# float64 weights converted by two bit operations and an integer addition, with one pair of heads masked on VectorE

## The chip, the cores and the metric

One core of a Trainium2 chip. The metric is the device time of one execution in microseconds. A core has five engines with queues of their own: TensorE (PE; its weight loads are listed as PEld), VectorE (DVE), ScalarE (ACT), GpSimd (POOL) and SyncE (SP).

## What is computed

Hashed attention, and behind it a Fourier mixing block, cut to what matters:

```python
# attention: B, H, S, D = 4, 8, 768, 64; float32
q_bits = einsum('bhsd,dk->bhsk', q, proj) > 0          # 6 bits; k_bits alike
mask   = q_bucket[:, :, :, None] == k_bucket[:, :, None, :]
scores = where(mask, q @ k.T / sqrt(D), -1e9)
attn   = exp(scores - max); attn = attn / (sum(attn) + 1e-09)
x      = (attn @ v), heads side by side: (4, 768, 512)
# mixing
u  = x + real(fft(fft(x, axis=1), axis=2))
un = (u - mean) / sqrt(var + 1e-06)
out = u + maximum(un @ w_ch1, 0.0) @ w_ch2             # (512, 2048) and (2048, 512)
```

`w_ch1` and `w_ch2` arrive as float64 (a float32 array times a float64 scalar); the rest is float32. The kernel is handed their 64-bit words and turns them into float32 itself.

## The kernel before, in words

**Attention.** Heads are taken in 16 pairs (`NPAIR` = 4 for each of 4 batches); a pair has six steps, one for each block of 128 keys (`NT` = 6). In each step `weigh` (L775 on) runs twice, for the two halves of the queries: TensorE computes scores of both heads (L789), ScalarE takes the exponential (L795) into one of four buffers `pk`. Then VectorE adds the new probabilities to the accumulators (L868), and TensorE multiplies the step before with the values (L809). After a pair, `scale` sums over the keys (L826) and divides on VectorE (L832 to L842).

The mask of equal buckets comes in one of two ways. For pairs in `LITE` (L541) the score matmul is led by two bf16 matmuls (L784) on the signs of the bits, scaled by 2^34, so that other buckets' exponentials vanish; the signs are prepared by wide matmuls (L727) and VectorE (L729, L734), and the copies of the transposed q and k all go to ScalarE (`act`, L692). For all other pairs `prepare` computes bucket numbers with narrow matmuls (L742, L754, L763), whose results go through score buffers in PSUM and are copied by VectorE and ScalarE in turn, and `weigh` multiplies each probability by "bucket of q equals bucket of k" on VectorE, two operations in a half step (L798). `prepare(n + 1)` runs inside pair n.

**Weights.** `weights` (L612) brings a 512-column slice at a time: 16 slices for w1 and 16 for w2. A slice's raw words are loaded (seven buffers for w1, three for w2; later loads are issued on GpSimd's queue, L636, when a buffer is free), then `narrow` (L581) converts it: three ScalarE operations make a mask of the values whose exponent fits float32 (L589 to L591), five VectorE operations shift the high word into place, set the exponent and sign, and turn the low word into a float remainder (L595, L598, L601, L605, L607), and GpSimd adds the remainder (L610). High and low words are read with a step of two. For w1, GpSimd also adds up four slices (L657), TensorE takes the mean (L670), and VectorE subtracts it (L673).

**Order.** In batch 0 the order of PE, DVE, ACT and POOL is that of the program (`manual_schedule`, L1034 on): one slice of w1 after each attention step, so the 16 slices lie in pairs 0 to 2. From batch 1 on a scheduler orders the instructions by its own costs; three steps of the mixing of the batch before follow each attention step, and from the eleventh mixing step of batch 0 on, slices of w2 alternate with mixing steps (L1065), during pairs 4 and 5.

**Mixing.** Per batch: sums and differences (L906, L910), channel transform (L923 and the copies L928, L930), sequence transform (L949, L965), two matmul layers (L974 with evictions L981 and L983; L1002), normalisation (L990 to L999) and stores (L893).

**The flag.** In the last batch the largest norms of q and k are reduced, transposed and compared (L1050 to L1060); if the exponentials could overflow, the kernel is followed by a general, slower version, `_any_scores`. With the given data it isn't run.

Of the kernel before, what the change touches and what calls it, by code (L numbers as in the profile page):

```python
# [23 lines left out]
DFF = 4 * DM  # L24
# [5 lines left out]
NDC = DM // P  # L30
GTT = 2
GT = GTT * P
WC = 512

SCALE = 1.0 / float(np.sqrt(D))
# [7 lines left out]
SAFE = 36.0  # L43
# [422 lines left out]
def _main(  # L466
# [9 lines left out]
    cn: dict,  # L476
):

    nc = tc.nc

    const = ctx.enter_context(tc.tile_pool(name="const", bufs=1))
# [11 lines left out]
    def wt(shape, dtype, tag, name, bufs=2):  # L493
        return work.tile(shape, dtype, tag=tag, name=name, bufs=bufs)
# [43 lines left out]
    make_identity(nc, ident)  # L538


    LITE = (0, 1, 2, 3, 4)  # L541
    pjw = const.tile([P, P], F32, tag="pjw", name="pjw")
    nc.gpsimd.memset(pjw, 0.0)
    for h in range(2):
# [15 lines left out]
    norms = const.tile([P, 2, NPAIR * B], F32, tag="norms", name="norms")  # L560
# [12 lines left out]
    w1 = const.tile([P, NDC, DFF], F32, tag="w1", name="w1")  # L573
# [7 lines left out]
    def narrow(dst, raw, mask):  # L581


        lo, hi = (raw.rearrange("p (n w) -> p n w", w=2)[:, :, i] for i in range(2))
        di, mi = dst.bitcast(I32), mask.bitcast(I32)

        nc.scalar.activation(mask, hi, AF.Abs)  # L589
        nc.scalar.activation(mask, mask, AF.Abs, bias=mid[:, 0:1])  # L590
        nc.scalar.activation(mi, mask, AF.Sign, bias=mid[:, 1:2])  # L591

        nc.vector.tensor_scalar(  # L595
            di, hi, 4, -(2**31), op0=ALU.logical_shift_left, op1=ALU.bitwise_xor
        )
        nc.vector.scalar_tensor_tensor(  # L598
            mi, di, 1, mi, op0=ALU.logical_shift_right, op1=ALU.bitwise_and
        )  # L600
        nc.vector.scalar_tensor_tensor(  # L601
            di, hi, -(2**31), mi, op0=ALU.bitwise_and, op1=ALU.bitwise_or
        )

        nc.vector.tensor_scalar(mi, di, -(1 << 23), None, op0=ALU.bitwise_and)  # L605
        rest = lo.bitcast(F32)
        nc.vector.scalar_tensor_tensor(  # L607
            rest, lo.bitcast(U32), 2.0**-52, mask, op0=ALU.mult, op1=ALU.mult
        )
        nc.gpsimd.tensor_tensor(dst, dst, rest, op=ALU.add)  # L610

    def weights(wsb, wdr):  # L612

        wide = wdr.dtype == I64
        slices = [
            (wsb[:, c, f : f + WC], wdr[c * P : (c + 1) * P, f : f + WC])
            for f in range(0, wdr.shape[1], WC)
            for c in range(wdr.shape[0] // P)
        ]
        raws, masks, adding = [], [], []  # L620
        if wide:
            zt = wt([P, 3, 2 * WC], F32, "z", f"zraw{wdr.shape[0]}", 1)
            raws += [zt[:, i] for i in range(3)]
            if wsb is w1:
                ft = wt([P, 12, WC], F32, "F", "fraw", 1)
                raws += [
                    ft[:, i : i + 2].rearrange("p i w -> p (i w)") for i in range(0, 8, 2)
                ]
                masks = [ft[:, i] for i in range(8, 12)]

        def fetch(i, queue):
            if i < len(slices):
                dst, src = slices[i]
                if wide:
                    raw = raws[i % len(raws)].bitcast(I32)
                    queue.dma_start(raw.bitcast(I64), src)  # L636
                else:
                    queue.dma_start(dst, src)

        depth = len(raws) or 4  # L640
        for i in range(depth):
            fetch(i, nc.sync if wsb is w1 else nc.gpsimd)
            if wsb is w1 and i == 1:
                load(1)
        yield
        for i, (dst, src) in enumerate(slices):
            if wide:
                mask = masks[i % 4] if masks else wt([P, WC], F32, "u", f"mask{i}", 2)
                narrow(dst, raws[i % len(raws)].bitcast(I32), mask)
# [37 lines left out]
    def prepare(n):  # L687

        lite = n in LITE
        act = lite and n > 0  # L692
# [349 lines left out]
    for b in range(B):  # L1042
        if b > 0:
            for _ in attention(b):
                for _ in range(per_step):
                    next(other, None)
        if b == B - 1:
            roomy[0] = True

            ms = const.tile([P, 2], F32, tag="ms", name="ms")  # L1050
            nc.vector.tensor_reduce(ms, norms, axis=AX.X, op=ALU.max)
            ps = pt([1, 2, P], "norms_t")
            for io in range(2):
                nc.tensor.transpose(ps[:, io, :], ms[:, io : io + 1], ident)
            mt = const.tile([1, 4], F32, tag="mt", name="mt")
            nc.vector.tensor_reduce(mt[:, 0:2], ps, axis=AX.X, op=ALU.max)
            nc.vector.tensor_tensor(mt[:, 2:3], mt[:, 0:1], mt[:, 1:2], op=ALU.mult)
# [55 lines left out]
```

## Time and profile before

| what | value |
|---|---|
| time, median of 3 runs | 1313.91 us (1313.45 to 1316.85) |
| the profiled execution | 1313.88 us, span 1312.0 us |
| PE busy | 1229.4 us (94%) |
| DVE busy | 691.7 us (53%) |
| ACT busy | 347.4 us (26%) |
| POOL busy | 138.1 us (11%) |
| moved by DMA | 44.65 MB, mean 34 GB/s |

Busy times overlap, as the engines run side by side, so they don't add up to the span. The page also gives the span in 40 slices, each digit the busy share in tenths. A row of a group gives line, engine, operation, output and inputs, shapes and count, then busy time, mean time of one in ns, and the idle time before with what ended it. A row of a stretch gives its start and end, its length, and for each engine the busy time and the number of instructions, then TensorE's granted clock (1.00 is full), the DMA share and GB/s.

### The profile page before, as it was taken

What the parts mean: (1) busy time and instruction counts of PE and PEld (TensorE: products, weight loads), DVE (VectorE), ACT (ScalarE), POOL (GpSimd) and SP (SyncE); (2) the same over time, 40 slices, a digit from 0 to 9 for tenths busy, and PEclk for the clock granted to TensorE, in tenths of its full rate; (3) what the DMA queues carried; (4) which work ended last, traced back from release to release, by engine and by line L of the source; (5) the groups of instructions that cost most, each with busy time, mean ns of one, the idle gap of its engine ahead of it and who ended that gap; (6) DMA issues with size and microseconds to landing.
All of it is one profiled execution on the core that took longest, in us unless ns stands there. A gap on an engine that the chain in (4) does not pass through costs nothing.

```text
span 1312.0 us, 12075 instructions
## 1 busy us (share of the span) xinstructions
PE 1229.4 (94%) x4688; PEld 619.9 (47%) x4688; DVE 691.7 (53%) x1184; ACT 347.4 (26%) x569; POOL 138.1 (11%) x183
## 2 busy tenths in 40 slices
PE   7657889899999999999999999999999998999997
PEld 3223356344445445644445444745445444854553
DVE  5999967994444448553444537653444635310010
ACT  6446444551122214122122213122112111110000
POOL 1443202430000100000100110000000000001000
PEclk9778999899999999999999999999999998999999
DMA  9321112330100101010110101010000000000000
GB/s 286 88 72 36 37 37 94 111 89 8 32 20 13 32 8 45 1 24 12 28 33 0 35 18 33 12 24 13 17 21 0 0 12 13 0 0 16 8 8 19
DMA packets 82881, 44.65 MB, mean 34 GB/s; under 512 B 76800, under 2 KB 76928, under 8 KB 82688
## 3 DMA queue, kind: packets, MB, share of 16 engines
q1 hardware_dynamic: 74032, 23.61, 7.2%
q0 software_dynamic: 5648, 19.40, 4.6%
q10 hardware_dynamic: 3136, 0.79, 0.3%
q8 instruction: 39, 0.64, 0.2%
q14 instruction: 26, 0.21, 0.1%
HBM read 37.50 MB, written 6.29 MB: 33 GB/s over the span
## 4 chain that ended last, share of the span: by engine, by line
PE 75%; DVE 17%; issue 4%; ACT 2%; DMA 1%; POOL 1%; SPq 0%; POOLq 0%; DVEq 0%; ACTq 0%
PE o L1002 24%; PE h L974 23%; PE sc L789 8%; PE oo L809 7%; DVE acc L868 4%; PE cs L923 3%; DVE pk L798 3%; PE B L949 2%; PE A L949 2%; DVE w L601 1%; PE sum L826 1%; DVE fraw L598 1%; ACT pk L795 1%; DVE zraw L607 1%; PE un L990 1%
## 5 line engine op out<-in xcount | busy, mean ns | idle before, releaser
L974 PE MATMUL h<-x,w 128*128 128x384 f32 x1024 | 344.4, 493 | 11.5 <-DVE rt L832 3.5
L1002 PE MATMUL o<-w,h 128*128 128x512 f32 x768 | 342.1, 597 | 0.4 <-DVE h L981 0.4
L974 PEld LDWEIGHTS h<-x,w 128*128 128x128 f32 x1024 | 192.1, 191 | 159.2 <-issue 12.8
L798 DVE SCALAR_TENSOR_TENSOR pk<-qb,kb,pk 128x384 f32<-128x384 bf16 x264 | 155.7, 628 | 189.3 <-ACT pk L795 189.3
L795 ACT ACTIVATE pk<-sc 128x768 f32<-128x768 f32 x192 | 149.2, 809 | 327.6 <-PE sc L789 250.6
L1002 PEld LDWEIGHTS o<-w,h 128*128 128x128 f32 x768 | 141.5, 190 | 174.2 <-issue 168.0
L789 PE MATMUL sc<-qt,kt 64*128 64x384 f32 x768 | 186.4, 518 | 2.8 <-ACT pk L795 2.8
L809 PE MATMUL oo<-pk,vn 128*64 128x384 f32 (+1 forms) x768 | 152.9, 500 | 1.7 <-ACT x L821 1.1
L868 DVE TENSOR_TENSOR acc<-acc,pk 128x768 f32<-128x768 f32 x128 | 134.9, 1063 | 5.2 <-ACT pk L795 3.4
L981 DVE TENSOR_SCALAR h<-h 128x384 f32<-128x384 f32 x64 | 35.6, 556 | 166.4 <-PE h L974 166.2
L789 PEld LDWEIGHTS sc<-qt,kt 64*128 64x128 f32 x768 | 77.5, 193 | 75.3 <-issue 49.9
L983 ACT ACTIVATE h<-h 128x384 f32<-128x384 f32 x64 | 31.4, 491 | 284.3 <-PE h L974 284.3
L1008 DVE SCALAR_TENSOR_TENSOR u<-o,rs,u 128x512 f32<-128x512 f32 x24 | 18.0, 750 | 150.5 <-PE o L1002 122.1
L809 PEld LDWEIGHTS oo<-pk,vn 128*64 128x64 f32 x768 | 48.1, 136 | 93.9 <-issue 79.0
L998 POOL TENSOR_SCALAR rs<-mv 128x1 f32<-128x1 f32 x24 | 6.5, 271 | 520.3 <-DVE mv L996 519.9
L923 PE MATMUL cs<-ch,z 128*128 128x256 f32 x192 | 49.2, 410 | 8.7 <-ACT qt L516 4.1
L893 POOL DMA_DIRECT2D out_dram<-u x32 | 19.7, 614 | 355.3 <-DVE u L1008 301.6
L610 POOL TENSOR_TENSOR w<-w,zraw 128x512 f32<-128x512 f32 x24 | 40.9, 1704 | 101.2 <-DVE zraw L607 98.1
L923 PEld LDWEIGHTS cs<-ch,z 128*128 128x128 f32 x192 | 37.9, 204 | 21.9 <-ACT qt L516 5.9
L992 ACT COPY u<-un 128x512 f32<-128x512 f32 x24 | 14.1, 588 | 114.5 <-PE un L990 114.5
L949 PE MATMUL B<-sq,F 128*128 128x193 f32 (+1 forms) x192 | 37.1, 329 | 1.4 <-DVE x L965 1.0
L949 PE MATMUL A<-sq,F 128*128 128x193 f32 (+1 forms) x192 | 37.4, 330 | 0.3 <-DVE x L965 0.3
(110 smaller groups left out, 901.1 us busy)
## 6 DMA issues: line engine op xcount, KB each, us to landing
zraw<-in_moe_w_ch_dram POOLq DMA_DIRECT2D x21, 512.0 KB, 3.9
qn<-in_q_dram SPq DMA_DIRECT2D x32, 192.0 KB, 3.1
vn<-in_v_dram SPq DMA_DIRECT2D x30, 192.0 KB, 3.2
kn<-in_k_dram SPq DMA_DIRECT2D x30, 192.0 KB, 3.2
out_dram<-u POOLq DMA_DIRECT2D x16, 256.0 KB, 2.4
fraw<-in_moe_w_ch_dram SPq DMA_DIRECT2D x4, 512.0 KB, 6.6
fraw<-in_moe_w_ch_dram POOLq DMA_DIRECT2D x4, 512.0 KB, 4.2
out_dram<-u POOLq DMA_DIRECT2D x16, 128.0 KB, 2.5
```

The source lines that it names most:

```text
L610: nc.gpsimd.tensor_tensor(dst, dst, rest, op=ALU.add)
L789: nc.tensor.matmul(ps[:, h, 0:HALF], kt[rows, ks], qt[rows, qs], start=kb is not None, stop=True,)
L795: nc.scalar.activation(pk[:, :, 0:HALF], ps[:, :, 0:HALF], AF.Exp, scale=SCALE)
L798: nc.vector.scalar_tensor_tensor(pk[:, h, 0:HALF], qb[:, h, qs], kb[:, h, c : c + 1], pk[:, h, 0:HALF], op0=ALU.is_equal, op1=ALU.mult,)
L809: nc.tensor.matmul(oos[g][h * D : (h + 1) * D, 0:w], nat["v", n][:, c, h, :], pk[g][:, h, 0:w], start=(c == 0), stop=(c == NT - 1),)
L868: nc.vector.tensor_tensor(accs[g], first[g][:, :, 0:HALF] if c == 1 else accs[g], new[g][:, :, 0:HALF], op=ALU.add,)
L923: nc.tensor.matmul(ps[:, pc:DM:2], z[:, cp, pc, par, t * P : (t + 1) * P], ch[:, cp, pc, :], start=(cp == 0), stop=(cp == 1),)
L949: nc.tensor.matmul(ps[:, cols], f, sq[:, t, k, cols], start=(t == 0), stop=(t == NT // 2 - 1),)
L974: nc.tensor.matmul(ps, w1[:, c, fc * P : (fc + 1) * P], x[:, c, g * HALF : (g + 1) * HALF], start=(c == 0), stop=(c == NDC - 1),)
L981: nc.vector.tensor_scalar(hr, ps, 0.0, None, op0=ALU.max)
L983: nc.scalar.activation(hr, ps, AF.Relu)
L1002: nc.tensor.matmul(ps, hs[fc][:, j * P : (j + 1) * P], w2[:, fc, :], start=(fc == 0), stop=(fc == NFC - 1),)
```

## The change

`narrow` keeps two VectorE operations: the high word shifted by three with the two top bits cleared, and the two top bits put back, which gives float32's bits cut off at the top of the low word. ScalarE scales the low word by 2^-29 into an integer from 0 to 8, and GpSimd adds that to the bits as integers, which rounds. This holds only for exponents in float32's normal range. So ScalarE checks the range: two Abs operations as before, then Relu with an accumulator in place of Sign, whose sum over the slice is kept in one of 32 columns of a new tile `strange` and is above zero if any value lies outside. The three write over the low words. In the last batch the largest of `strange` joins the flag, which can call the general version. Pair 4 leaves `LITE`: it is masked on VectorE and prepared as pairs 5 to 15 are.

```diff
-    LITE = (0, 1, 2, 3, 4)
+    LITE = (0, 1, 2, 3)
...
+    strange = const.tile([P, 2 * NDC * DFF // WC], F32, tag="strange", name="strange")
+    nc.gpsimd.memset(strange, 0.0)
+
+    def narrow(dst, raw, low, col):
         lo, hi = (raw.rearrange("p (n w) -> p n w", w=2)[:, :, i] for i in range(2))
-        di, mi = dst.bitcast(I32), mask.bitcast(I32)
-        nc.scalar.activation(mask, hi, AF.Abs)
-        nc.scalar.activation(mask, mask, AF.Abs, bias=mid[:, 0:1])
-        nc.scalar.activation(mi, mask, AF.Sign, bias=mid[:, 1:2])
+        di = dst.bitcast(I32)
         nc.vector.tensor_scalar(
-            di, hi, 4, -(2**31), op0=ALU.logical_shift_left, op1=ALU.bitwise_xor
+            di, hi, 3, (1 << 30) - 1,
+            op0=ALU.logical_shift_left, op1=ALU.bitwise_and,
         )
         nc.vector.scalar_tensor_tensor(
-            mi, di, 1, mi, op0=ALU.logical_shift_right, op1=ALU.bitwise_and
-        )
-        nc.vector.scalar_tensor_tensor(
-            di, hi, -(2**31), mi, op0=ALU.bitwise_and, op1=ALU.bitwise_or
-        )
-        nc.vector.tensor_scalar(mi, di, -(1 << 23), None, op0=ALU.bitwise_and)
-        rest = lo.bitcast(F32)
-        nc.vector.scalar_tensor_tensor(
-            rest, lo.bitcast(U32), 2.0**-52, mask, op0=ALU.mult, op1=ALU.mult
-        )
-        nc.gpsimd.tensor_tensor(dst, dst, rest, op=ALU.add)
+            di, hi, -(1 << 30), di, op0=ALU.bitwise_and, op1=ALU.bitwise_or
+        )
+        nc.scalar.activation(low, lo.bitcast(U32), AF.Copy, scale=2.0**-29)
+        nc.gpsimd.tensor_tensor(di, di, low, op=ALU.add)
+        t = lo.bitcast(F32)
+        nc.scalar.activation(t, hi, AF.Abs)
+        nc.scalar.activation(t, t, AF.Abs, bias=mid[:, 0:1])
+        nc.scalar.activation(
+            t, t, AF.Relu, bias=mid[:, 1:2], accum_out=strange[:, col : col + 1]
+        )
...
-            ms = const.tile([P, 2], F32, tag="ms", name="ms")
-            nc.vector.tensor_reduce(ms, norms, axis=AX.X, op=ALU.max)
-            ps = pt([1, 2, P], "norms_t")
-            for io in range(2):
+            ms = const.tile([P, 3], F32, tag="ms", name="ms")
+            nc.vector.tensor_reduce(ms[:, 0:2], norms, axis=AX.X, op=ALU.max)
+            nc.vector.tensor_reduce(ms[:, 2:3], strange, axis=AX.X, op=ALU.max)
+            ps = pt([1, 3, P], "norms_t")
+            for io in range(3):
                 nc.tensor.transpose(ps[:, io, :], ms[:, io : io + 1], ident)
...
+            nc.vector.tensor_scalar(
+                mt[:, 4:5], mt[:, 3:4], (SAFE / SCALE) ** 2, None, op0=ALU.is_gt
+            )
             fl = const.tile([1, 1], I32, tag="fl", name="fl")
-            nc.vector.tensor_scalar(fl, mt[:, 2:3], (SAFE / SCALE) ** 2, None, op0=ALU.is_gt)
+            nc.vector.scalar_tensor_tensor(
+                fl, mt[:, 2:3], 0.0, mt[:, 4:5], op0=ALU.is_gt, op1=ALU.max
+            )
```

More of the change, by code (lines that the diff above doesn't have):

```diff
@@ L579, in _main @@
     nc.gpsimd.memset(mid[:, 1:2], -float((127 << 20) + 64))
-    def narrow(dst, raw, mask):
+    strange = const.tile([P, 2 * NDC * DFF // WC], F32, tag="strange", name="strange")
+    nc.gpsimd.memset(strange, 0.0)
+    def narrow(dst, raw, low, col):
         lo, hi = (raw.rearrange("p (n w) -> p n w", w=2)[:, :, i] for i in range(2))
-        di, mi = dst.bitcast(I32), mask.bitcast(I32)
-        nc.scalar.activation(mask, hi, AF.Abs)
-        nc.scalar.activation(mask, mask, AF.Abs, bias=mid[:, 0:1])
-        nc.scalar.activation(mi, mask, AF.Sign, bias=mid[:, 1:2])
+        di = dst.bitcast(I32)
         nc.vector.tensor_scalar(
-            di, hi, 4, -(2**31), op0=ALU.logical_shift_left, op1=ALU.bitwise_xor
+            di, hi, 3, (1 << 30) - 1,
+            op0=ALU.logical_shift_left, op1=ALU.bitwise_and,
         )
         nc.vector.scalar_tensor_tensor(
-            mi, di, 1, mi, op0=ALU.logical_shift_right, op1=ALU.bitwise_and
+            di, hi, -(1 << 30), di, op0=ALU.bitwise_and, op1=ALU.bitwise_or
         )
-        nc.vector.scalar_tensor_tensor(
-            di, hi, -(2**31), mi, op0=ALU.bitwise_and, op1=ALU.bitwise_or
-        )
-        nc.vector.tensor_scalar(mi, di, -(1 << 23), None, op0=ALU.bitwise_and)
-        rest = lo.bitcast(F32)
-        nc.vector.scalar_tensor_tensor(
-            rest, lo.bitcast(U32), 2.0**-52, mask, op0=ALU.mult, op1=ALU.mult
-        )
-        nc.gpsimd.tensor_tensor(dst, dst, rest, op=ALU.add)
+        nc.scalar.activation(low, lo.bitcast(U32), AF.Copy, scale=2.0**-29)
[5 more added lines that the diff above has]
+            t, t, AF.Relu, bias=mid[:, 1:2], accum_out=strange[:, col : col + 1]
+        )
     def weights(wsb, wdr):
@@ L648, in weights @@
                 mask = masks[i % 4] if masks else wt([P, WC], F32, "u", f"mask{i}", 2)
-                narrow(dst, raws[i % len(raws)].bitcast(I32), mask)
+                narrow(
+                    dst, raws[i % len(raws)].bitcast(I32), mask.bitcast(I32),
+                    i if wsb is w1 else len(slices) + i,
+                )
             fetch(i + depth, nc.gpsimd)
@@ L1048, in _main @@
             roomy[0] = True
-            ms = const.tile([P, 2], F32, tag="ms", name="ms")
-            nc.vector.tensor_reduce(ms, norms, axis=AX.X, op=ALU.max)
-            ps = pt([1, 2, P], "norms_t")
-            for io in range(2):
-                nc.tensor.transpose(ps[:, io, :], ms[:, io : io + 1], ident)
-            mt = const.tile([1, 4], F32, tag="mt", name="mt")
-            nc.vector.tensor_reduce(mt[:, 0:2], ps, axis=AX.X, op=ALU.max)
-            nc.vector.tensor_tensor(mt[:, 2:3], mt[:, 0:1], mt[:, 1:2], op=ALU.mult)
+            ms = const.tile([P, 3], F32, tag="ms", name="ms")
[3 more added lines that the diff above has]
+            for io in range(3):
+                nc.tensor.transpose(ps[:, io, :], ms[:, io : io + 1], ident)
+            mt = const.tile([1, 5], F32, tag="mt", name="mt")
+            nc.vector.tensor_reduce(mt[:, 0:3], ps, axis=AX.X, op=ALU.max)
+            nc.vector.tensor_tensor(mt[:, 3:4], mt[:, 0:1], mt[:, 1:2], op=ALU.mult)
+            nc.vector.tensor_scalar(
+                mt[:, 4:5], mt[:, 3:4], (SAFE / SCALE) ** 2, None, op0=ALU.is_gt
+            )
             fl = const.tile([1, 1], I32, tag="fl", name="fl")
-            nc.vector.tensor_scalar(fl, mt[:, 2:3], (SAFE / SCALE) ** 2, None, op0=ALU.is_gt)
+            nc.vector.scalar_tensor_tensor(
+                fl, mt[:, 2:3], 0.0, mt[:, 4:5], op0=ALU.is_gt, op1=ALU.max
+            )
             large = nc.values_load(fl[0:1, 0:1], min_val=0, max_val=1)
```

## The prediction

> **What bounds the kernel now.** I read the page's slices first, then the busy times by stretch, then the chain of waits inside the first stretch, then the groups of instructions there.
>
> ```profile
> PE   7657889899999999999999999999999998999997
> ...
> DVE  5999967994444448553444537653444635310010
> ```
>
> TensorE is full from the tenth slice (32.8 us each) to the end; only before it is there something to win, and there VectorE shows nines twice. I cut that part at the first scores of each pair of heads.
>
> ```profile
> core 0: us, PE busy (x) PEld busy (x) DVE busy (x) ACT busy (x) POOL busy (x), PEclk, DMA share, GB/s
> 13.40:57.90 44.50, 32.48 (x164) 13.39 (x166) 39.13 (x53) 28.63 (x47) 18.72 (x15) 0.87 0.62 196
> 57.90:111.70 53.80, 35.97 (x177) 15.36 (x176) 50.16 (x71) 28.42 (x47) 20.83 (x15) 0.82 0.23 62
> 111.70:147.30 35.60, 27.87 (x129) 11.45 (x130) 33.84 (x50) 18.23 (x29) 13.40 (x7) 0.87 0.13 29
> 147.30:171.20 23.90, 23.14 (x137) 10.26 (x136) 21.36 (x36) 14.61 (x26) 0.00 (x0) 1.00 0.18 41
> 171.20:206.00 34.80, 31.23 (x166) 19.91 (x164) 20.12 (x36) 12.67 (x21) 2.22 (x7) 0.95 0.21 55
> 206.00:229.70 23.70, 21.61 (x120) 15.97 (x120) 21.28 (x40) 13.08 (x19) 6.09 (x6) 1.00 0.29 102
> 229.70:297.00 67.30, 57.85 (x211) 27.93 (x210) 64.65 (x106) 36.10 (x58) 27.24 (x23) 0.95 0.32 97
> 330.00:1290.00 960.00, 946.37 (x3437) 480.46 (x3436) 421.57 (x763) 185.49 (x305) 43.39 (x82) 1.00 0.07 17
> ```
>
> The rows are pairs 0, 1 and 2 (all 16 slices of w1 are converted in them), pair 3 (no conversion), and then pair 4 and most of pair 5 with the 16 slices of w2. Pair 3 shows what TensorE alone needs for a pair: 23.9 us at full clock. Pairs 0 to 2 took 133.9 us in place of some 70, with VectorE busy for 39.13 + 50.16 + 33.84 = 123.1 us. The chain says the same:
>
> ```profile
> 66.60 2.83 DVE acc L868 x2
> ...
> 72.47 2.83 DVE acc L868 x2
> ```
>
> From one pair of accumulations to the next, 5.87 us, every piece of the chain is VectorE's: the five operations of one slice and the two accumulations. Stage two (171.2 to 297) is mixed: TensorE idles 3.6 + 2.1 + 9.4 = 15.1 us of 125.8, mostly in the last row, where VectorE is busy for 64.65 of 67.3. After 330 TensorE idles 13.6 us of 960, and VectorE is under half busy; nothing that the change does to VectorE can matter there.
>
> **The change, part by part.**
>
> *Three of five VectorE operations go (w1).* In the stretch 13.4 to 147.3:
>
> ```profile
> L598 DVE SCALAR_TENSOR_TENSOR fraw<-w,fraw 128x512 int32<-128x512 int32 x16 | 12.9, 803 | 5.5 <-ACT fraw L591 4.0
> ...
> L605 DVE TENSOR_SCALAR fraw<-w 128x512 int32<-128x512 int32 x16 | 6.8, 427 | 0.5
> ...
> L607 DVE SCALAR_TENSOR_TENSOR zraw<-zraw,fraw 128x512 f32<-128x512 uint32 x8 | 5.6, 695 | 0.3
> L607 DVE SCALAR_TENSOR_TENSOR fraw<-fraw 128x512 f32<-128x512 uint32 x8 | 5.5, 694 | 0.3
> ```
>
> The two that stay have the forms of L595 and L601, so I take 12.9 + 6.8 + 5.6 + 5.5 = 30.8 us off VectorE, which leaves 92.3. It also no longer waits for ScalarE's mask; the one wait of 4.0 us (first row) goes.
>
> *ScalarE gets a fourth operation and a read of the accumulator.* Its stream in one step:
>
> ```profile
> 73.91 1.49 ACT L795 ACTIVATE pk<-sc 128x768 f32<-128x768 f32 x2
> 75.29 0.84 ACT L682 ACTIVATE sq<-kn 128x768 bf16<-128x768 f32 x1
> 76.02 0.20 ACT L682 ACTIVATION_READ_ACCUMULATOR sq<-kn 128x1 f32 x1
> 76.11 0.67 ACT L589 ACTIVATE fraw<-zraw 128x512 f32<-128x512 int32 x1
> 76.81 0.72 ACT L590 ACTIVATE fraw<-fraw,mid 128x512 f32<-128x512 f32 x1
> 77.57 0.72 ACT L591 ACTIVATE fraw<-fraw,mid 128x512 int32<-128x512 f32 x1
> 78.20 1.49 ACT L795 ACTIVATE pk<-sc 128x768 f32<-128x768 f32 x2
> ```
>
> The two Abs stay, Relu stands for Sign (0.72), the scaled copy of the low words is new; I price it as L589, which also reads every second word (0.67), and the read at 0.20: 0.87 a slice, 13.9 in all, so ScalarE goes from 28.63 + 28.42 + 18.23 = 75.3 to 89.2 us in the stretch. The copy's form on unsigned words is in no row; 0.67 to 0.72 bounds it. So the next-latest engine is ScalarE, not TensorE. A step like the one above takes ScalarE 78.20 - 73.91 = 4.29 us, afterwards 5.16; VectorE's step falls from 5.87 to about 4.0. Where a step has a norm or the copies of the next pair (steps 1 to 3 of a pair, about 8 of the 16 with a slice), ScalarE now sets the pace and 1.16 us of the gain is lost, 9.3 in all if nothing evens out. Four probability buffers let it run one step ahead; I take 6 lost. Stage one then gains 30.8 - 6 = 25 us. Ends: 17 if the added operation comes in full at each slice (30.8 - 13.9), 35 if nothing is lost and the 4.0 us go as well.
>
> *The range check is queued behind the copy.* Exponentials of the next step stand behind these three operations; that is in the 5.16. On GpSimd the fetch of a later slice now waits for Relu too, as it overwrites the raw words; behind it stands the next add. With seven raw buffers for w1 that fetch is far ahead of its use, and GpSimd is busy for 53 of 133.9 us: nothing. For w2 there are three buffers, which is one reason why I count little there.
>
> *The add on GpSimd is of integers.*
>
> ```profile
> L610 POOL TENSOR_TENSOR w<-w,zraw x24: 1278/1663/2344, 21.0 to 294.6; 128x512 f32<-128x512 f32 x24
> ```
> ```profile
> 153.18 1.82 DVE L868 TENSOR_TENSOR acc<-pk,pk 128x768 f32<-128x768 f32 x2
> ```
>
> No row has an integer add; I take the same time (1.28 us undisturbed), since its operands are as many and as wide, with 0.6 and 2.6 (half and double) as bounds. A longer one also costs VectorE: two accumulations take 1.82 us with GpSimd idle and 2.83 beside an add, so 1.0 us goes per add of about 1.7. Doubled adds would thus cost VectorE about 16 x 1.3 x 0.6 = 12 us in stage one, and the sum would end near 1293; halved ones would give back some 6. The Trainium skill (SBUF — State Buffer, "SBUF: two separate sides") says that VectorE's two-input operations and GpSimd share a port pair under an exclusive lock and that the loser blocks for the whole instruction. By that rule a doubled add would cost the full 16 x 1.3 = 21 us, and the sum would end near 1302; the trace is milder than the rule, 1.0 us lost to an add that never takes under 1.28.
>
> *w2.* In 206 to 297:
>
> ```profile
> L598 DVE SCALAR_TENSOR_TENSOR mask<-w,mask 128x512 int32<-128x512 int32 x16 | 14.6, 910 | 0.1
> L798 DVE SCALAR_TENSOR_TENSOR pk<-qb,kb,pk 128x384 f32<-128x384 bf16 x16 | 13.5, 868 | 1.7 <-ACT pk L795 1.7
> ...
> L607 DVE SCALAR_TENSOR_TENSOR zraw<-zraw,mask 128x512 f32<-128x512 uint32 x16 | 11.0, 687 | 0.3
> ...
> L605 DVE TENSOR_SCALAR mask<-w 128x512 int32<-128x512 int32 x16 | 7.3, 454 | 0.1
> ```
>
> 14.6 + 11.0 + 7.3 = 32.9 us leave VectorE. *Pair 4 masked on VectorE* adds 24 operations as L798, 0.868 here, so at most 20.8 us; the first four of its six steps lie in 171 to 206, where VectorE idles 14.7 us. Over the stage VectorE goes from 106 to at most 94 of 125.8, ScalarE from 61.9 to 75.8. TensorE drops the 24 bf16 matmuls:
>
> ```profile
> 171.25 0.34 PE L784 MATMUL sc<-qkb 64*128 64x384 bf16 x2
> 171.42 0.81 PE L789 MATMUL sc<-qt,kt 64*128 64x384 f32 x4
> ```
>
> Two of them hold the queue for 0.17 us, so 12 x 0.17 = 2.0 us. Pair 4's preparation, inside pair 3, swaps four wide sign matmuls for narrow ones and three trips through the score buffers: one gains, the other stalls; nothing. TensorE's values of a step now wait for a mask that is queued behind conversion work on VectorE; mix work stands between, but I charge 1.5 us. Of the 15.1 us idle I give back half, 7.5, because two engines that are three quarters busy still come late at times. Stage two gains 7.5 + 2.0 - 1.5 = 8 us; ends 0 (ScalarE's longer bursts delay the evictions as much as VectorE's relief helps) and 17 (15.1 + 2.0).
>
> *The flag.* A third small transpose and two more tiny operations ahead of the load of the flag; TensorE waited for it
>
> ```profile
>   PE cs L923: 0.8, 1
> ```
>
> so I add 0.5 us. Everything from 297 on has the same instructions: nothing, or 3 us either way from a shifted order.
>
> **The sum.** The profiled execution took 1313.88 us (span 1312.0 and 1.9 around it), the median is 1313.91, so both serve: 1313.9 - 25 - 8 + 0.5 = 1281.
>
> **The rivals.**
>
> *ScalarE takes the place of VectorE.* Both added costs come in full: 17 us in stage one, about 1 in stage two: 1296. For it: 89.2 against 92.3 us of work in one stretch, in order, each feeding the other. Against it, ScalarE's own waits in the stretch:
>
> ```profile
> ACT pk L795 <- PE sc L789: 35.3, 9, 14.6
> ```
>
> It waited 35 us for scores that came late, so it has room. The Trainium skill (ScalarE: Activation LUTs, "Rules for kernel authors") would have relu and multiplications on VectorE, not ScalarE; that rule speaks for this rival. Chance 0.2.
>
> *Nothing is lost.* 35 in stage one and 17 in stage two: 1262. For it: clocks of 0.82 to 0.87 in pairs 0 to 2 that would rise. Chance 0.16.
>
> *GpSimd becomes the bound, slower.* Its other work is (53 - 16 x 1.66) / 16 = 1.6 us a slice. It sets stage one if the add takes over 133.9 / 16 - 1.6 = 6.8 us, five times the float one. At 10 us, 16 x 11.6 = 186 us: 52 more than now, 1366 at least. Only an integer path of another kind could do that. Chance 0.04.
>
> *It doesn't do what it says.* The 24 adds in L610's row show that the weights do come as 64-bit words, so the edit is live; a gain eaten up elsewhere, within 0.3% (3.9 us, about what a measurement can tell), gets 0.02.
>
> **The numbers.** Forecast 0.58, so faster 0.58 + 0.2 + 0.16 = 0.94, same 0.02, slower 0.04. The range joins both ends: 1313.9 - 52 = 1262 to 1313.9 - 17 = 1297.
>
> **What would show it.** VectorE in stage one at 92 to 97 us; pair 3's first scores near 122 us in place of 147.3; first waits of exponentials and fetches behind ScalarE's check; integer adds of 1.3 to 2 us; TensorE idle under 10 us in stage two; from there the same length as before. Wrong if the integer adds exceed 3 us, if pair 4's values wait for masks by more than 5 us in all, or if stage one keeps its length with ScalarE full.

## The result, and the profile after

The changed kernel takes 1284.97 us (median of 4 runs, 1284.52 to 1285.68), the kernel before 1314.92 us (4 runs, 1313.45 to 1316.85): ratio 0.9772, 95% interval 0.9755 to 0.9789. That is 30 us less, of 33 forecast, inside the range of 1262 to 1297. The profiled execution has a span of 1283.1 us (before: 1312.0).

First the slices of the page, changed kernel:

```profile
PE   6878898999999999999999999999999998999997
...
DVE  3988888734446366443454448554434635311110
```

All but one of VectorE's nines are eights now, and TensorE's low stretch is shorter by one slice. Busy times by stretch, cut where the prediction cut them (first scores of pair 3, first scores of pair 4, first output matmul), and behind them the row of the kernel before for the last of these stretches, which is the only one that the prediction did not show in this cut:

```profile
core 0: us, PE busy (x) PEld busy (x) DVE busy (x) ACT busy (x) POOL busy (x), PEclk, DMA share, GB/s
13.50:122.60 109.10, 89.86 (x466) 38.70 (x467) 90.50 (x126) 87.84 (x154) 49.63 (x37) 0.91 0.40 120
122.60:148.13 25.53, 21.74 (x147) 9.45 (x147) 21.43 (x36) 13.92 (x24) 0.00 (x0) 1.00 0.17 39
148.13:278.40 130.27, 120.55 (x509) 67.20 (x508) 97.05 (x163) 74.66 (x134) 30.50 (x36) 0.99 0.28 83
```
```profile
171.20:307.30 136.10, 119.87 (x532) 68.51 (x531) 110.11 (x186) 64.20 (x102) 35.55 (x36) 0.96 0.26 80
```

Stage one (pairs 0 to 2, all of w1) took 133.9 us and takes 109.1: 24.8 us less. VectorE did 123.1 us of work there and does 90.5; ScalarE did 75.3 and does 87.8. Pair 3, with no conversion in it, got longer, 23.9 to 25.5 us. Stage two (to the first output matmul) took 136.1 us and takes 130.3: 5.8 us less, with TensorE idle for 9.7 us of it in place of 16.2. From the first output matmul to the end it is 1312.0 - 307.3 = 1004.7 us before and 1283.1 - 278.4 = 1004.7 us after. So the whole gain is made ahead of 278 us: 24.8 - 1.6 + 5.8 = 29.0, the 28.9 by which the spans differ.

The integer addition, as a group in the changed kernel (w1):

```profile
L600 POOL TENSOR_TENSOR w<-w,fraw 128x512 int32<-128x512 int32 x16 | 26.3, 1642 | 64.0 <-DVE w L595 28.9 <-ACT fraw L599 22.6 <-DMA kn<-in_k_dram 4.6
```

Mean 1642 ns, and 1259 ns for the shortest. The float additions of w1 in the kernel before:

```profile
L610 POOL TENSOR_TENSOR w<-w,zraw 128x512 f32<-128x512 f32 x8 | 15.4, 1924 | 46.7 <-DVE zraw L607 43.6 <-ACT fraw L589 3.1
L610 POOL TENSOR_TENSOR w<-w,fraw 128x512 f32<-128x512 f32 x8 | 14.1, 1768 | 41.1 <-DVE fraw L607 34.0 <-DVE vs L818 7.0
```

Now one step of pair 0 in the changed kernel, ScalarE's instructions in order of time:

```profile
30.70 1.49 ACT L795 ACTIVATE pk<-sc 128x768 f32<-128x768 f32 x2
32.09 0.84 ACT L682 ACTIVATE sq<-kn 128x768 bf16<-128x768 f32 x1
32.82 0.20 ACT L682 ACTIVATION_READ_ACCUMULATOR sq<-kn 128x1 f32 x1
32.91 0.68 ACT L599 ACTIVATE fraw<-fraw 128x512 int32<-128x512 uint32 x1
33.62 0.69 ACT L603 ACTIVATE fraw<-fraw 128x512 f32<-128x512 int32 x1
34.34 0.77 ACT L604 ACTIVATE fraw<-fraw,mid 128x512 f32<-128x512 f32 x1
35.14 0.80 ACT L605 ACTIVATE fraw<-fraw,mid 128x512 f32<-128x512 f32 x1
35.82 0.19 ACT L605 ACTIVATION_READ_ACCUMULATOR fraw<-fraw,mid 128x1 f32 x1
```

There is no gap, and the next exponentials start at 35.91: the step is 35.91 - 30.70 = 5.21 us of ScalarE's own work (forecast for such a step: 5.16). In pair 0 VectorE waits for these exponentials, as the view of waits from 13.6 to 49.6 us says (total, times, longest):

```profile
DVE acc L868 <- ACT pk L795: 11.2, 4, 5.0
```

The theory with which the experiments began: pair 0 is now bound by ScalarE, pairs 1 and 2 by VectorE, and stage two gained less than hoped because of pair 4's move to VectorE or of what the conversions still cost there.

### The profile page after: what moved, and what is told of

Same layout as the page of the kernel before. It is cut to its first block, busy times and chain, and to the rows that moved or that the text cites. A ratio compares the mean times of both kernels' runs of the same rounds, so it can differ in the third digit from the quotient of the medians.

```text
span 1283.1 us, 12028 instructions
## 1 busy us (share of the span) xinstructions
PE 1221.6 (95%) x4675; PEld 615.9 (48%) x4675; DVE 646.0 (50%) x1114; ACT 369.5 (29%) x631; POOL 129.8 (10%) x184
## 4 chain that ended last, share of the span: by engine, by line
PE 78%; DVE 12%; DMA 3%; ACT 3%; issue 3%; POOL 0%; SPq 0%; ACTq 0%; POOLq 0%; DVEq 0%
PE h L974 25%; PE o L1002 25%; PE sc L789 9%; PE oo L809 7%; DVE pk L798 3%; PE cs L923 3%; DVE acc L868 3%; PE B L949 2%; PE A L949 2%; DMA zraw<-in_moe_w_ch_dram 2%; ACT pk L795 1%; PE sum L826 1%; DVE w L595 1%; PE un L990 1%; PE trk L701 1%
## 5 line engine op out<-in xcount | busy, mean ns | idle before, releaser
L798 DVE SCALAR_TENSOR_TENSOR pk<-qb,kb,pk 128x384 f32<-128x384 bf16 x288 | 169.3, 626 | 194.1 <-ACT pk L795 194.1
L809 PE MATMUL oo<-pk,vn 128*64 128x384 f32 (+1 forms) x768 | 157.5, 501 | 0.8 <-DVE pk L798 0.8
L868 DVE TENSOR_TENSOR acc<-pk,pk 128x768 f32<-128x768 f32 x32 | 32.0, 1020 | 5.3 <-ACT pk L795 5.0
```

Of the source, the lines that this page charges most:

```text
L798: nc.vector.scalar_tensor_tensor(pk[:, h, 0:HALF], qb[:, h, qs], kb[:, h, c : c + 1], pk[:, h, 0:HALF], op0=ALU.is_equal, op1=ALU.mult,)
L809: nc.tensor.matmul(oos[g][h * D : (h + 1) * D, 0:w], nat["v", n][:, c, h, :], pk[g][:, h, 0:w], start=(c == 0), stop=(c == NT - 1),)
L868: nc.vector.tensor_tensor(accs[g], first[g][:, :, 0:HALF] if c == 1 else accs[g], new[g][:, :, 0:HALF], op=ALU.add,)
```

## The experiments

So that they can be compared, this table gives the length of each pair in each profile, in us: from 13.5 to the end of pair 0, from there to the end of pair 1, and so on; "two" is from the end of pair 3 to the first output matmul. The end of a pair is taken where `scale` begins on VectorE, at the copy `vs` (L818); that is up to some 8 us behind TensorE's last value matmul of the pair, as VectorE is late there. "Same again" is the changed kernel once more, unaltered, in the series of e9 to e11. What follows "two" is 1003.9 to 1005.0 us in all of them. Each ratio is to runs of the kernel before in the same series (medians 1311.87 to 1314.92 us).

| kernel | pair 0 | pair 1 | pair 2 | pair 3 | two | median, us | ratio to before, 95% |
|---|---|---|---|---|---|---|---|
| before | 41.6 | 50.8 | 38.9 | 24.6 | 137.9 | 1314.92 | 1 |
| after | 33.7 | 39.1 | 33.3 | 26.8 | 132.1 | 1284.97 | 0.9772 (0.9755 to 0.9789) |
| same again | 33.9 | 38.9 | 31.5 | 28.4 | 131.2 | 1283.19 | 0.9777 (0.9764 to 0.9790) |
| e1 | 33.9 | 38.9 | 31.5 | 25.2 | 133.2 | 1283.33 | 0.9779 (0.9763 to 0.9794) |
| e2 | 41.4 | 50.8 | 39.8 | 28.0 | 135.3 | 1313.49 | 1.0001 (0.9988 to 1.0013) |
| e3 | 28.7 | 38.8 | 33.3 | 28.3 | 133.8 | 1280.23 | 0.9738 (0.9717 to 0.9759) |
| e4 | 35.9 | 38.5 | 32.8 | 28.2 | 129.7 | 1286.01 | 0.9794 (0.9778 to 0.9811) |
| e5 | 35.5 | 41.3 | 32.9 | 27.9 | 133.7 | 1290.54 | 0.9837 (0.9816 to 0.9859) |
| e6 | 33.1 | 34.5 | 30.9 | 28.6 | 125.8 | 1272.27 | 0.9691 (0.9668 to 0.9714) |
| e7 | 27.7 | 38.4 | 33.5 | 28.7 | 132.0 | 1282.01 | 0.9767 (0.9749 to 0.9784) |
| e8 | 33.6 | 38.9 | 31.5 | 28.2 | 131.1 | 1283.47 | 0.9783 (0.9765 to 0.9801) |
| e9 | 27.6 | 38.2 | 33.8 | 28.6 | 132.9 | 1282.19 | 0.9765 (0.9752 to 0.9779) |
| e10 | 43.0 | 55.3 | 43.2 | 28.2 | 126.5 | 1314.22 | 1.0015 (1.0006 to 1.0024) |
| e11 | 28.2 | 38.0 | 31.4 | 29.4 | 125.1 | 1272.37 | 0.9685 (0.9671 to 0.9698) |

The two executions of the unaltered kernel show how far a single cell can be trusted: pairs 2 and 3 differ by 1.8 and 1.6 us with the granted clock (0.90 and 1.00 against 0.95 and 0.94), and their sum by 0.1. So pairs 2 and 3 are read as a sum below. Stage two differs by 0.9 us between them, by 1.0 between e7 and e9, which are one kernel, and in e4, which only adds work on ScalarE, it is 2.4 us shorter; so differences of up to some 2.5 us there are not taken as shown effects.

> The changed kernel once more, unaltered, so that the late check below has it in the same call. Both theories: ratio to the kernel before 0.977 as measured (0.975 to 0.979).

The ratio came out as before, 0.9777.

**Pair 4 (e1, e2).** e1 is the changed kernel with pair 4 back in `LITE`; e2 is the kernel before with pair 4 taken out of it and nothing else changed.

```diff
 # e1, against the changed kernel
-    LITE = (0, 1, 2, 3)
+    LITE = (0, 1, 2, 3, 4)
 # e2, against the kernel before
-    LITE = (0, 1, 2, 3, 4)
+    LITE = (0, 1, 2, 3)
```

> The new conversion, but pair 4 back in LITE (masked by the bf16 matmuls as before). My theory: pair 4's move is worth next to nothing. In the changed kernel pair 3 takes 25.6 us from its first scores to pair 4's, 1.6 more than before, since pair 4's preparation is copied by VectorE too and makes three trips through the score buffers; the bf16 matmuls that it saves in pair 4 are 2.0 us. So 1283 to 1287 us, with pair 3 back at 24 us and pair 4 some 2 us longer. Rival 1: the masks on VectorE ate the four us by which stage two missed the forecast; then this kernel takes about 1281. Rival 2: the move is what earned the gain after pair 3; then about 1290.

> The old conversion, with pair 4 masked on VectorE: the other half of the change alone. My theory: with five VectorE operations a slice, VectorE is busy 64.65 of 67.3 us in the stretch from 229.7 to 297 of the kernel before, and pair 4's 24 masks come on top; what does not fit into the 14.7 us that it idles in 171 to 206 shows: 1317 to 1322 us, 3 to 8 more than before. Rival (the move costs nothing whatever the conversion): 1313 to 1316. Either way pairs 0 to 2 take 134 us as before.

e1's ratio is that of the changed kernel. e2's is 1.0001: my expectation of a slower kernel was wrong, although VectorE is then busy for 121.07 of 135.34 us in stage two:

```profile
173.46:308.80 135.34, 126.86 (x519) 69.81 (x516) 121.07 (x214) 64.83 (x104) 37.13 (x36) 0.95 0.26 80
```

The move is worth nothing, with or without the new conversion, so the gain is the conversion's; but not because nothing happens. Pairs 0 to 2 agree to 0.1 us in e1 and in the unaltered kernel run again, so their rows from pair 3's first scores (first row) and from pair 4's (second) can be set side by side. First e1, then the unaltered kernel:

```profile
120.79:144.76 23.97, 23.20 (x137) 10.27 (x137) 21.52 (x36) 14.50 (x26) 0.00 (x0) 1.00 0.18 41
144.76:276.10 131.34, 120.98 (x533) 69.64 (x532) 82.30 (x139) 74.73 (x134) 31.42 (x36) 0.96 0.27 83
```
```profile
120.83:148.02 27.19, 23.39 (x147) 9.97 (x146) 21.66 (x36) 14.37 (x24) 0.00 (x0) 0.94 0.16 37
148.02:277.40 129.38, 121.29 (x509) 67.48 (x508) 95.48 (x163) 74.50 (x134) 30.52 (x36) 0.97 0.27 84
```

Pair 3, in which pair 4 is prepared, is 3.2 us longer with the move (at a granted clock of 0.94 in place of 1.00), and stage two 2.0 us shorter. In the first profile of the changed kernel, at 1.00 as before, pair 3 is longer by 1.6 us than before, and its stage two 1.1 us shorter than e1's. The first is in every run: pair 3 takes 24.6 and 25.2 us in the two kernels without the move, and 26.8 to 29.4 in all others. The gain in stage two is not clear of the differences there. TensorE's waits in pair 3, as its timeline in the changed kernel shows them:

```profile
128.64 0.55 PE L701 MATMUL trq<-ident,qn 128*128 128x128 f32 x3 [2.34 <-DVE w L673]
...
141.81 0.24 PE L763 MATMUL kb<-pw,bt 32*128 32x2 bf16 x6 [1.11 <-DVE qb L515]
```

The first is a transpose put behind the last of w1's mean subtractions, the second a step of the narrow preparation.

**Which engine sets the pace (e3, e4, e5).** e3 leaves out the range check, three ScalarE operations a slice; e4 doubles one of them; e5 adds a VectorE operation that changes nothing.

```diff
 # e3
-        nc.scalar.activation(t, hi, AF.Abs)
-        nc.scalar.activation(t, t, AF.Abs, bias=mid[:, 0:1])
-        nc.scalar.activation(
-            t, t, AF.Relu, bias=mid[:, 1:2], accum_out=strange[:, col : col + 1]
-        )
 # e4, behind the second Abs
+        nc.scalar.activation(t, t, AF.Abs)
 # e5, behind the first bit operation
+        nc.vector.tensor_scalar(di, di, -1, None, op0=ALU.bitwise_and)
```

> The changed kernel without the range check: the three ScalarE operations and the accumulator's read are left out, so out-of-range weights would not be noticed. My theory: ScalarE sets the pace of pair 0 (busy 33.0 of 36.0 us there, and VectorE waits 11.2 us for exponentials), VectorE that of pairs 1 and 2. Taking 2.9 us a slice off ScalarE gains 5 to 8 us in pair 0, 1 to 2 in the other two, 0 to 2 in stage two: 1274 to 1279 us. Rival (VectorE and its adds beside GpSimd still set all three pairs): 1283 or more. Rival (ScalarE holds stage two as well): under 1272, with the stretch from pair 4's first scores to the first output matmul 5 us shorter or more.

> The changed kernel with one more Abs per slice on ScalarE (the value is positive already, so the result stays): the suspected cost doubled, 0.78 us a slice. If ScalarE sets the pace of pair 0 alone, six slices make 4 to 5 us there and the other ten 0 to 2: 1289 to 1292 us. If ScalarE sets it in all of stage one: 16 x 0.78 = 12.5, about 1297. If it never does: 1285 to 1286.

> The changed kernel with one more bit operation per slice on VectorE (an and with all ones, some 0.42 us, so the result stays). If VectorE sets pairs 1 and 2 and ScalarE pair 0: nothing in pair 0 (its six slices are hidden), 10 x 0.45 = 4 us in pairs 1 and 2, 0 to 2 in stage two, so 4 to 6 us over the changed kernel's 0.977 of before: about 0.981. If the order of TensorE's work, not VectorE's load, decides stage two, nothing of it shows there. Rival (VectorE still sets all of stage one): 7 us, 0.983, with pair 0 longer by 2.7.

In e3 pair 0 falls from 33.7 to 28.7 us and nothing else gets shorter by more than 0.3; in e4 pair 0 rises by 2.2 us, pair 1 falls by 0.6 and pairs 2 and 3 together rise by 1.0. So ScalarE holds pair 0 and hardly anything else. Both did less than expected: e3's 1280.23 us lie above the 1274 to 1279 of the theory, and e4's 1286.01 below the 1289 to 1292 for a bound in pair 0, as six operations made that pair 2.2 us longer and not 4 to 5. In e5 pair 0 rises by 1.8 and pair 1 by 2.2 us, pairs 2 and 3 together by 0.7, stage two by 1.6: 6.4 us in the profile and 0.0065 of the ratio (8.5 us) in time for 32 operations, about the total that the rival gave, but spread otherwise than it said. VectorE is still on the path in pair 1 and in part of pair 0; for stage two e5's 1.6 us don't show it, but e6 does. The 5.0 us of e3 do not all arrive: pairs 2 and 3 together are 1.6 and stage two 1.7 us longer in its profile, which is that of the slowest of its four executions (1275.95 to 1283.04 us). The timed gain against the changed kernel is 0.0034 of the ratio (4.5 us), with intervals that overlap at their ends.

**What the addition costs VectorE (e6).** The integer addition is left out, so the weights are cut off and not rounded to float32.

```diff
-        nc.gpsimd.tensor_tensor(di, di, low, op=ALU.add)
```

> The changed kernel without GpSimd's integer add (the weights are then cut off rather than rounded; ScalarE still scales the low words, unread). It shows what the add costs VectorE through the port that the two share: two accumulations take 2.82 us beside an add and 1.83 alone. If that contention is what VectorE loses in pairs 1 and 2: some 1.0 us a slice over ten slices, so 5 to 9 us less there, pair 0 unchanged within 1 us because ScalarE sets it. The ratio to before falls from 0.977 to about 0.971. Rival (contention is absorbed elsewhere): 0.976 to 0.978.

The profiles differ by 12.0 us, the ratios by 0.0081 (10.6 us), with intervals that lie apart: 0.6 us are in pair 0, 4.6 in pair 1, 0.6 in pairs 2 and 3, 6.3 in stage two. GpSimd was not full of additions (POOL 30.5 of 130 us), and no wait of TensorE in stage two is put down to one; they act through VectorE. The groups of VectorE in stage two, the changed kernel first, then e6 (L797 there is L798 here):

```profile
L798 DVE SCALAR_TENSOR_TENSOR pk<-qb,kb,pk 128x384 f32<-128x384 bf16 x42 | 28.1, 701 | 7.4 <-ACT pk L795 7.4
...
L595 DVE SCALAR_TENSOR_TENSOR w<-zraw,w 128x512 int32<-128x512 int32 x16 | 11.9, 748 | 0.3
L591 DVE TENSOR_SCALAR w<-zraw 128x512 int32<-128x512 int32 x16 | 10.8, 683 | 4.1 <-DMA zraw<-in_moe_w_ch_dram 4.1
```
```profile
L797 DVE SCALAR_TENSOR_TENSOR pk<-qb,kb,pk 128x384 f32<-128x384 bf16 x42 | 24.2, 608 | 10.5 <-ACT pk L794 10.4
...
L595 DVE SCALAR_TENSOR_TENSOR w<-zraw,w 128x512 int32<-128x512 int32 x16 | 10.9, 687 | 0.2
L591 DVE TENSOR_SCALAR w<-zraw 128x512 int32<-128x512 int32 x16 | 6.6, 417 | 4.0 <-DMA zraw<-in_moe_w_ch_dram 4.0
```

The same operations, as many of each: a mask takes 701 ns on the mean in the kernel with additions and 608 in the one without, the first bit operation 683 and 417, the second 748 and 687. That is 3.9 + 4.2 + 1.0 = 9.1 us of VectorE's time in stage two alone. VectorE waits as long for loaded words in both (4.1 and 4.0 us), so earlier loads are not what e6 gains.

**Heads apart (e8).** In pair 4 each head's mask now releases its own value matmul. The group of value matmuls in stage two, e1 first (pair 4 without masks), then the changed kernel:

```profile
L809 PE MATMUL oo<-pk,vn 128*64 128x384 f32 (+1 forms) x84 | 15.9, 498 | 0.0
```
```profile
L809 PE MATMUL oo<-pk,vn 128*64 128x385 f32 (+1 forms) x84 | 20.1, 503 | 0.3 <-DVE pk L798 0.3
```

Some 84 x 0.5 = 42 us of matmuls lie on 15.9 us there and on 20.1 here: as many, as long, but fewer of them overlap with another. e8 makes both heads of pair 4 wait for the last mask of the step:

```diff
+                if n == NPAIR:
+                    tc.add_manual_dep(
+                        mm.ins, masked[n, 1, c].ins.name,
...
+                        reason="values of a step together",
+                    )
```

> The changed kernel, where in pair 4 every value matmul of a step waits for the last of that step's four masks, so that the scheduler can't put a single head's value matmuls between other work. In the changed kernel the value matmuls keep TensorE busy 20.1 us from the end of pair 3 to the first output matmul, with pair 4 in LITE 15.9, as two heads run side by side in two halves of the columns only when they follow each other. If these lone heads are what ate the 2 to 4 us that the dropped bf16 matmuls should have given: that figure falls to 16 or 17 and the stretch from 132.1 to 128 to 130 us, ratio 0.974 to 0.976. Rival (lone heads fill gaps that would be idle anyway): the busy time falls, the stretch stays within 1.5 us.

```profile
L810 PE MATMUL oo<-pk,vn 128*64 128x385 f32 (+1 forms) x84 | 18.1, 501 | 2.8 <-DVE pk L799 2.8
```

The busy time falls by 2.0 us, half of what the theory asked for, and 2.8 us of waiting takes its place; stage two is 1.0 us and 0.1 us shorter than in the two profiles of the changed kernel, and the ratio is 0.9783. The rival is right: a head that came alone filled time in which TensorE would have waited for the other.

**The check five slices later (e7, e9).** The check writes over the raw words, so a slice can be checked at any time before its buffer is loaded anew. e7 and e9 (one kernel, run in two series) check slice i - 5 of w1 behind slice i, which takes the check out of most of pair 0.

```diff
+        late = 5 if wide and wsb is w1 else 0
...
+                narrow(dst, raws[i % len(raws)].bitcast(I32), mask.bitcast(I32))
+                if i >= late:
+                    check(raws[(i - late) % len(raws)].bitcast(I32), base + i - late)
+            if i >= late:
+                fetch(i - late + depth, nc.gpsimd)
```

> The changed kernel with w1's range check five slices behind the conversion (all checks are still made; the raw buffer of slice i is refetched after its check, so five steps later). Pair 0 then has one check in place of six, pair 1 and 2 as many as now, the last five come in pairs 2 and 3, where ScalarE idles. If ScalarE's burden in pair 0 is what the change left behind, pair 0 gets as short as without the check, 42.2 in place of 47.2 us for the end of its last values, and the whole 3 to 5 us less than the changed kernel, ratio 0.973 to 0.975. Rival (the checks cost as much wherever they stand): the gain of pair 0 comes back as a loss in pairs 1 to 3, ratio 0.977.

> The late check once more, unaltered, beside the changed kernel in the same call. Theory (ScalarE's three check operations a slice delay pair 0's exponentials, which is what e3 got 4 to 5 us for): ratio lower than the changed kernel's of the same call by 0.002 to 0.004 (3 to 5 us), pair 0 again about 6 us shorter. Rival (what pair 0 wins is given back by a changed order behind the first batch, as e7's timed runs suggest): the two ratios are equal within 0.001.

Pair 0 falls to 27.7 and 27.6 us (28.7 in e3). Timed, little is left: 0.9765 (1280.48 to 1282.79 us) beside 0.9777 (1282.72 to 1284.38 us) of the unaltered kernel in one series, 1.0 us between the medians, between theory and rival and nearer to the rival. Pairs 2 and 3 give back 2.5 us (62.4 for 59.9), where the moved operations now stand. Pair 2 in the unaltered kernel, then in e9:

```profile
86.29:117.78 31.49, 26.73 (x146) 11.48 (x144) 30.31 (x42) 25.45 (x45) 17.66 (x11) 0.95 0.17 39
```
```profile
79.31:113.12 33.81, 27.77 (x152) 12.07 (x150) 30.97 (x42) 30.36 (x56) 19.13 (x14) 0.95 0.33 95
```

ScalarE does 30.36 us in place of 25.45. Stage two is 1.7 us longer, as in e3; whether that is an effect of either edit stays open.

**A third VectorE operation in place of the addition (e10, e11).** Instead of ScalarE's copy and GpSimd's addition, VectorE ORs the low word's top bits in (cut off, not rounded). e11 has the late check as well.

```diff
-        nc.scalar.activation(low, lo.bitcast(U32), AF.Copy, scale=2.0**-29)
-        nc.gpsimd.tensor_tensor(di, di, low, op=ALU.add)
+        nc.vector.scalar_tensor_tensor(
+            di, lo, 29, di, op0=ALU.logical_shift_right, op1=ALU.bitwise_or
+        )
```

> The changed kernel without the copy on ScalarE and without the integer add on GpSimd: a third VectorE operation ORs the low word, shifted right by 29, into the bits, so the weights are cut off and not rounded to float32. Theory (what is left on the path is ScalarE in pair 0 and, in pairs 1, 2 and stage two, the 1 us that each GpSimd add takes from VectorE): a slice costs VectorE 0.69 us more and 1.0 us less, and ScalarE 0.68 us less, so pair 0 gains 3 to 4 us, pairs 1 and 2 together 1 to 3, stage two 2 to 4: ratio near 0.972. Rival (VectorE's own operations set the pace, and an operation more on it costs what the added one of e5 cost, 7 us in all, as much as the add's removal gave in e6 from pair 1 on): ratio 0.976 to 0.978, pairs 1 and 2 no shorter.

> e10's third VectorE operation (weights cut off, not rounded) and e9's late check together. Theory: the two relieve different pairs; pair 0 has no check and no copy left in front of its exponentials and comes near the 27 us that e3 and e7 show as the floor by VectorE, the rest is as in e10: ratio 0.969 to 0.971. Rival (the first pair's gain is given back later, as in e7): ratio as e10's within 0.001.

e10 missed both expectations: 1314.22 us, as slow as the kernel before. Pairs 0 to 2 take 141.4 us in place of 104.3. Its chain of waits in pair 0 shows why (pieces of 0.2 us and less are left out):

```profile
33.17 1.83 DVE acc L868 x2
...
36.63 0.34 DVE w L591
37.00 0.70 DVE w L595
37.73 0.70 DVE w L599
38.45 0.66 ACT fraw L604
39.14 0.75 ACT fraw L605
39.94 0.62 issue
40.75 0.71 ACT pk L795
41.48 4.15 DVE acc L868 x2
```

It is a ring: the accumulations wait for exponentials; VectorE's three operations stand behind the accumulations (and here behind the next pair's signs, L729 and L734); ScalarE's check may write over the low words only once the third of them has read them; and the next exponentials stand behind the check. In the changed kernel only ScalarE's own copy reads the low words, so the check waits for nobody. The wait as the view of waits has it, e10, pairs 0 to 2:

```profile
ACT fraw L604 <- DVE w L599: 38.2, 8, 8.2
ACT zraw L604 <- DVE w L599: 22.8, 7, 5.2
```

61.0 us in which ScalarE stood with exponentials queued behind it. e11 settles that this is the cause: the same operations with the check five slices later take 97.6 us in pairs 0 to 2, and the wait is gone; 1272.37 us, 10.8 us under the unaltered kernel of that series. Its ratio, 0.9685, is just under what the theory expected of e11. Stage two is short in both, 126.5 and 125.1 us, as in e6 (125.8), and 129.7 to 133.8 in every version of the changed kernel that has the additions. Against e9, which has the same late check, e11 loses 0.6 us in pair 0 and gains 0.2 in pair 1, 1.6 in pairs 2 and 3 and 7.8 in stage two: in pairs 0 and 1 the third operation costs about what the copy and the addition cost, as the rival for e10 said, and nearly all of the gain lies in stage two.

## Why the prediction was right, point by point

- **Stage one gains 25** (ends 17 and 35): 24.8. The busy times hold: VectorE went from 123.1 to 90.5 us (forecast 92.3; just under the 92 to 97 named as a sign), ScalarE from 75.3 to 87.8 (89.2). ScalarE's loss of 6 us is right in total, 30.8 - 24.8 = 6.0, but was put at about 8 of 16 steps, and most of it lies in pair 0. By the table, pair 0 gains 7.9 us of the 11.6 that its six slices take off VectorE, pair 1 11.8 of 11.6, and pair 2, with four slices, 5.6 of 7.7 (7.4 in the second profile). No run takes out just what ScalarE got in addition, so the 6 itself was not measured: e4 shows that one operation more costs pair 0 2.2 us, e3 that the whole check, three operations of which the kernel before had the like, costs it 5.0. That a choice between 0 and 9.3 came out to a microsecond is partly luck. In pairs 1 and 2 VectorE, with mean subtractions and additions beside it, is still the later one (e5 and e6 move pair 1, e3 and e4 hardly do).
- **A cut of the prediction is misplaced**: 111.70 is the second step of pair 2, whose first scores are at 103.81. Only sums over pairs 0 to 2 are used, so nothing hangs on it.
- **The integer addition takes the time of the float one**: 1642 ns on the mean beside VectorE's work (the float ones of w1 1924 and 1768), and 1.26 to 1.29 us undisturbed (1.28). Right.
- **The fetch behind Relu costs nothing**: GpSimd does wait for the check before fetches, 3.4 us in stage one and 10.8 in stage two, and VectorE waits 4.1 us for loaded words in stage two. In e3, without the check, this last wait is 1.2 us and stage two is no shorter, so no cost shows; the fetch was not tried alone.
- **Pair 3 near 122 us**: 122.6. **Same length behind the first output matmul**: 1004.7 us both. **TensorE idle under 10 us in stage two**: 9.7. **Values of pair 4 wait for masks by no more than 5 us**: 0.3. Right.
- **Stage two gains 8** (ends 0 and 17): 5.8 - 1.6 = 4.2. This is the step that was mis-sized, in two of its terms, half of the idle time and the preparation. *Half of the idle time, 7.5*: e1, which has the new conversion and not the move, gains 136.1 - 131.3 = 4.8. The half was a choice, and the idle time was taken for VectorE's load; e1 has only 82.30 us of that in 131.34 and ends no earlier than the changed kernel with 95.48 in 129.38, while e6 and e11, with the additions gone, are faster there by 5 to 7. The additions, which the change keeps, thus hold more than the 2.7 us that are missing. *The dropped bf16 matmuls, 2.0, less 1.5 for masks that come late*: against e1 the move shortens stage two by 1.1 and 2.0 us in the two profiles, which fits the 0.5 forecast as well as more. The value matmuls' 4.2 us more, which the prediction did not see, fill time in which TensorE would have waited (e8), and its busy time, 120.55 us for 119.87 before, did not fall. *Pair 4's preparation inside pair 3, nothing*: 1.6 us in the profile after, 3.2 in the other. In the first profile these add up to the 4.2 but for rounding: 4.8 + 1.1 - 1.6. The move thus pays for itself and no more, which the ratios of e1 and e2 confirm.
- **The flag, 0.5 us**: not to be seen in 1004.7 us on both sides.
- **A doubled addition would cost VectorE 0.6 of its length**: the rows of the last section speak against this reading, though the sum did not hang on it. A longer addition was not tried.
- **The rivals.** *ScalarE takes over* is what happens in pair 0, and hardly elsewhere. *Nothing is lost* failed in pair 0 and in stage two. *GpSimd as the bound* and *no effect* did not occur.

## What to carry to other kernels

When an engine on the path is relieved, read the next-latest engine for each stage, not over the sum: here ScalarE was next in one pair of three, and the rest stayed with VectorE and with the GpSimd work that shares its access. Before an operation that only checks or cleans up is put into an in-order queue, ask what it overwrites and who reads that last: one more reader on VectorE made the check close a ring, and with the check five slices later the same kernel was 42 us faster. A matmul group whose busy time rises while its count and mean stay the same has lost overlap; here that cost nothing, as TensorE would have waited in that time (e8).

## What the runs showed of the hardware

In the changed kernel a VectorE operation that begins inside a GpSimd addition is held until about the end of that addition, even where it reads one tensor and the addition has just begun, unless one of its inputs lies in PSUM, where the matmuls' results land (the other operands lie in SBUF). From the timelines of the changed kernel in stage two, GpSimd first, then VectorE:

```profile
199.08 1.27 POOL L600 TENSOR_TENSOR w<-w,mask 128x512 int32<-128x512 int32 x1 [0.62 <-DVE w L595]
...
201.53 1.27 POOL L600 TENSOR_TENSOR w<-w,mask 128x512 int32<-128x512 int32 x1 [0.68 <-DVE w L595]
...
226.29 1.29 POOL L600 TENSOR_TENSOR w<-w,mask 128x512 int32<-128x512 int32 x1
```
```profile
199.57 1.07 DVE L591 TENSOR_SCALAR w<-zraw 128x512 int32<-128x512 int32 x1 [0.58 <-DMA zraw<-in_moe_w_ch_dram]
...
202.22 1.01 DVE L965 TENSOR_TENSOR x<-x,B 128x384 f32<-128x384 f32 x2
...
226.48 1.40 DVE L591 TENSOR_SCALAR w<-zraw 128x512 int32<-128x512 int32 x1 [0.69 <-DMA zraw<-in_moe_w_ch_dram]
```

The first and the last of these additions end at 200.35 and 227.58, the bit operations at 200.64 and 227.88: 0.29 and 0.30 us later, although one began 0.49 and the other 0.19 us into the addition; alone such an operation takes 0.42. The two operations of L965, which read a matmul's result in PSUM, meet the middle addition and take 1.01 us together, 0.55 each with a little overlap; so they do in e6, without additions. In that profile 32 VectorE operations begin inside one of the conversion's additions. The 24 with all operands in SBUF, of eight forms, end 0.03 to 0.82 us after the addition, each some 0.1 to 0.2 us less than such an operation takes alone; the 8 that read PSUM (L965 and L515) take as long as alone, 0.55 and 0.96 us. In the kernel before, 3 of 33 such operations were not held; why is open. A held operation loses nearly all that is left of the addition and not a share of it. That a pair of accumulations lost only 1.0 us, on which the prediction built its 0.6, does not contradict this: the first of the two began ahead of the addition and went on, and the second was held for the rest only. The addition is then the longer one, 1.85 us and not 1.27. The Trainium skill (SBUF — State Buffer, "SBUF: two separate sides") states such an exclusive lock between GpSimd and a VectorE operation that has two inputs in SBUF or runs in a two-port mode, taken by whichever starts first, for the whole instruction; these rows agree with it, though no run here shows in which mode the one-input operations ran.

The second and third of the range check's operations on ScalarE take 0.77 and 0.80 us, where they read and write every second word in place; those of the mask before, in a tile without gaps, took 0.72 each.
